# A four-heads-a-step layout for one attention block, together with new scheduler settings, in a kernel of two attention blocks

## The chip, the cores and the metric

The kernel runs on one core of one Trainium2 chip. The metric is the device time of one execution in microseconds (us); lower is better. A kernel's time is the median of its runs.

Names used below: PE is the matmul engine and PEld its weight loads, ACT the activation engine, DVE the vector engine, POOL a fourth engine, SP the engine that issues the DMAs (loads and stores), and SPq its queue. PSUM is the memory of the tiles that the matmuls here write (ps_... in the views), SBUF the on-chip memory of the program's other tiles. The "page" of a run is a summary of the hardware profile of one execution, its "span" the time from the first to the last instruction, and the "granted clock" the share of full speed at which PE was let run.

## The reference

Two attention blocks with separate inputs; their outputs are concatenated. Block A has 32 query heads that share 4 key/value heads, block B has 32 heads with their own keys and values. B holds eight times A's cache, and it is the block that the change touches.

```python
# A: B, Sq, D, Hq, Hkv, Sk, Dh = 16, 32, 1024, 32, 4, 1024, 128   (bf16)
# B: B, Sq, D, H,  Sk, Dh      = 16, 32, 1024, 32,    1024, 128   (bf16)
def _B_ref(x, k_cache, v_cache, wq, wo):
    q = (x @ wq).reshape(B, Sq, H, Dh).transpose(0, 2, 1, 3)
    scores = jnp.einsum("bhqd,bhkd->bhqk", q, k_cache) * (Dh ** -0.5)
    p = softmax(scores, axis=-1)
    o = jnp.einsum("bhqk,bhkd->bhqd", p, v_cache)
    return o.transpose(0, 2, 1, 3).reshape(B, Sq, H * Dh) @ wo
# A is the same with k and v repeated 8 times along the head axis
return jnp.concatenate([a, b], axis=-1)          # (16, 32, 2048)
```

## The kernel before

The program does not issue instructions directly. Every operation is recorded with what it reads and writes, and a **list scheduler** then simulates the recorded program and fixes the order of instructions on each engine. That order is final, and the chip keeps to it: in the trace of the kernel before, DVE's 884 recorded operations and ACT's 725 started in the order of the program. An engine whose next entry is not ready waits, as DVE did for 46.3 us in all before the transposes of K. The simulation has its own picture of the chip: a table of durations, an assumed data rate `DMA_BW` (bytes per us), a latency for a signal between engines, a margin before a DMA may be issued, and a window `look` within which two candidates count as equally early.

```python
A_STEPS_FRAC = 0.92            # A's steps are spread over this part of B's steps
DMA_BW = 330.7e3               # the model's data rate: 330.7 GB/s
DMA_MARGIN = {"kb_dma": 0.5, "vb_dma": 0.5, "ka_dma": 0.5, "va_dma": 0.5}
DMA_MARGIN_DEFAULT = 2.0
DUR = {"scoresB": 1.1, ..., "exp": 1.25, ..., "KBt_tr": 1.15, ...}      # us each, cut

def list_schedule(self, lat=0.12, dma_bw=DMA_BW, dma_lat=1.8, look=0.35):
    ...   # pick the engine and operation that can start first; within `look`, the longest path to the end
            if op.dma_key is not None:                    # a load or store
                xs = max(st + 0.06, dma_free[0])
                dma_free[0] = xs + op.dur / dma_bw        # op.dur is bytes here
                op.t1 = dma_free[0] + dma_lat             # when the model sees it landed
            else:
                op.t1 = st + op.dur
            for u in users[best]:                         # what waits for it
                r = op.t1 + (0.0 if same_pe else lat)
                if uo.dma_key is not None:
                    r += DMA_MARGIN.get(uo.name, DMA_MARGIN_DEFAULT)
                ...
```

B is worked in 128 steps. A step takes two batches and two heads, 1 MiB of K and 1 MiB of V. K has two slots in SBUF and V three. A step transposes K on DVE (two transposes of 128x1024, 1223 ns each), multiplies with 32x32 PE tiles into a score buffer in PSUM, takes exp with the row sums in one ACT instruction (in the trace 1029 ns, and 200 ns for reading the accumulator), transposes the result on PE, multiplies with V and normalises. A runs 128 steps of its own between them, and the projections x@wq and the output projections are mixed in. The two score buffers rotate over A's and B's steps alike, in the order in which the steps are recorded.

```python
def quadB_all(q):
    st_ktrB(q, 0); st_ktrB(q, 1)                        # DVE transposes of K, free its slot
    if t + NKB < NIT: st_dmaK(quadsB[t + NKB])           # load of K two steps ahead
    if t >= 1 and t - 1 + NVB < NIT: st_dmaV(quadsB[t - 1 + NVB])
    st_scores(q); st_exp(q); st_ptr(q); st_pev(q, "act"); st_pv(q); ...

# K of a step: every partition gets two runs of 4 KB (t is one of two batches, hh one of two heads)
ksrc = pb["k"][q.b0:q.b0+2, q.h0:q.h0+2].rearrange("t hh (p s) d -> (hh p) t (s d)", s=16)

# score buffers
q.sbuf = sbuf_rr[0] % 2

# Q of B: project, transpose on DVE, shuffle on PE into the operand layout, and evacuate on ACT
last = e.matmul(ps_pj[:, 0:CW], xT_sb[:, 1, j, G*P:(G+1)*P], wq_sb[:, 1, j, :], ...)
pr.add("dve", lambda e: e.transpose(QBt..., Qtok...), name="QBt_tr")
for rg in range(4):
    e.matmul(ps_pj[32*rg:32*rg+32, ...], ident[32*a:32*a+32, 32*a:32*a+32], rhs, tile_position=(32*a, 32*rg))
evac(QR[:, gp, a, :, :], ps_pj[:, 0:2*Dh]..., name="QR_ev", eng="act")
```

`ps_pj` is one PSUM bank that all projections, the output projections and this shuffle share.

## Time and profile before

The kernel's three runs before the prediction had a median of 917.7 us (912.47 to 920.21).

| what | value |
|---|---|
| bytes moved | 341.64 MB |
| mean rate over the span | 375 GB/s |
| PE busy | 783.4 us, 86% of the span |
| ACT, DVE busy | 462.1 and 519.3 us |
| first 100 us | 308 GB/s |
| 100 to 840 us | 388 GB/s |

The page of the kernel before: the span, the busy time of each engine with its instructions, the rate in 40 equal slices of the span, the DMA total, the DMA queue (packets, MB, and the time of its packets as a share of 16 engines' span), and the chain of work that ended last.

```profile
span 911.5 us, 28186 instructions
...
PE 783.4 (86%) x12610; PEld 432.9 (47%) x12610; DVE 519.3 (57%) x891; ACT 462.1 (51%) x853; POOL 67.9 (7%) x76
...
GB/s 333 270 302 370 308 399 361 402 385 390 359 380 409 411 349 400 401 381 392 368 405 403 411 374 390 375 346 397 405 408 399 385 398 403 333 409 397 385 410 190
DMA packets 151934, 341.64 MB, mean 375 GB/s; under 512 B 10496, under 2 KB 26880, under 8 KB 151808
...
q1 hardware_dynamic: 151808, 339.78, 97.6%
...
PE 56%; ACT 14%; DVE 13%; DMA 12%; issue 2%; SPq 2%; POOL 0%; POOLq 0%; DVEq 0%; ACTq 0%
...
```

Two readings compete here. PE is busy for 86% of the span and makes up 56% of the chain that ended last, which looks like a PE-bound kernel. But its best slices move 411 GB/s, and at that rate 341.6 MB take 831 us (341.6 / 411, an estimate), so most of the 911.5 us is data time, with slices at 270 to 375 GB/s between the good ones.

The costliest groups of the kernel before that the change touches: line, engine, operation, output <- inputs with shapes and count | busy us, mean ns of one | idle us just before, and what ended most of it.

```profile
L848 DVE STREAM_TRANSPOSE KBt_sb<-KB_sb 128x1024 f32<-128x1024 f32 x256 | 306.6, 1223 | 46.3 <-DMA KB_sb<-in_B_k_cache_dram 22.6
L887 PE MATMUL ps_s<-KBt_sb,QR 32*32 32x512 bf16 x4096 | 167.0, 402 | 13.8 <-ACT P_sb L907 7.4
...
L907 ACT ACTIVATE P_sb<-ps_s 128x1024 bf16<-128x1024 f32 x128 | 131.7, 1029 | 70.3 <-PE ps_pt L921 36.5
...
L588 ACT CAST QR<-ps_pj 128x256 bf16<-128x256 f32 x128 | 48.5, 379 | 46.0 <-PE ps_pj L694 43.3
...
```

The same view with shapes kept apart has the Q shuffle itself on PE: 43.9 us, and 17.5 us of idle time before its matmuls.

```profile
...
L694 PE MATMUL ps_pj<-QBt,ident 32*32 32x256 bf16 x512 | 43.9, 287 | 17.5 <-ACT QR L588 10.0 <-DVE acc L748 2.6 <-DVE Qtok L590 1.5
...
```

Stretches of the kernel before: start:end, length, busy us and count of PE, PEld, DVE, ACT, POOL, then granted clock, DMA share, GB/s.

```profile
0.00:100.00 100.00, 77.32 (x800) 37.64 (x800) 34.88 (x56) 34.78 (x58) 6.45 (x16) 0.86 0.85 308
100.00:840.00 740.00, 657.45 (x10953) 371.86 (x10946) 446.98 (x772) 403.54 (x741) 61.38 (x59) 0.98 1.01 388
840.00:900.00 60.00, 45.39 (x843) 22.22 (x821) 34.93 (x57) 23.55 (x54) 0.00 (x0) 0.91 0.99 381
900.00:911.50 11.50, 3.21 (x43) 1.19 (x43) 2.48 (x8) 0.27 (x1) 0.10 (x1) 0.79 0.14 52
```

The DMA queue's own waits in the kernel before (what it waited for: us in total, times, longest). Line 813 is the load of K.

```profile
SPq L813 <- DVE KBt_sb L848: 220.4, 64, 13.0
...
```

And the waits of the engines: the K transposes on DVE waiting for K to land.

```profile
...
DVE KBt_sb L848 <- DMA KB_sb<-in_B_k_cache_dram: 22.6, 22, 2.3
...
```

A load of K cannot be issued before the slot's old contents have been transposed. Here the queue stood still for 220 us waiting for that, while the transposes themselves waited for their data for only 23 us.

The view names the DVE instruction that signalled last before the issue of the load was over, and an issue of a load of K took 0.37 us in the median (line 813), in the case below long enough for the next instruction in DVE's list to start before it and end during it. One case from the timeline of the kernel before (start, length, engine, line; other engines cut):

```profile
...
781.56 2.35 DVE L848 STREAM_TRANSPOSE KBt_sb<-KB_sb 128x1024 f32<-128x1024 f32 x2
...
783.83 0.39 DVE L949 TENSOR_TENSOR OA_sb<-ps_kt,rinv_all 128x256 bf16<-128x256 f32 x1
783.94 0.37 SPq L813 DMA_DIRECT2D KB_sb<-in_B_k_cache_dram  x1
...
```

The load starts 0.03 us after the second transpose ends (783.91), after 5.0 us of waiting, and in the program it depends on no other DVE instruction; but the view puts this wait down to line 949. So two counts are taken from the times in the traces here, load by load. The first is the queue's idle time just before loads of K: 329 us in the kernel before, all but 0.3 us of it ended by the transpose that frees the slot. The second is how long landed K waits for the start of its first transpose (a load has landed when its last signal shows in the trace): 221 us, added up over the 128 loads.

### The profile page before, as it was taken

To read this page: it belongs to the slowest core of one execution; us is meant where nothing else is said; L and a number is where in the kernel's file an instruction comes from. 1 tells how busy PE (TensorE), PEld (TensorE's weight loads), DVE (VectorE), ACT (ScalarE), POOL (GpSimd) and SP (SyncE) were. 2 spreads that over 40 slices of the span, in tenths; PEclk is the share of its full clock that TensorE was granted. 3 is DMA by queue.
4 is the path that set the end of the run, shared out by engine and by line. 5 is a ranking of instruction groups with operands and counts; after the bars stand their busy time and mean duration, and the time that the engine had idled before them with its cause. 6 is when DMAs were issued, how large, how long until landed. Compare 5 with 4: busy or idle time off the path is not lost.

```text
span 911.5 us, 28186 instructions
## 1 busy us (share of the span) xinstructions
PE 783.4 (86%) x12610; PEld 432.9 (47%) x12610; DVE 519.3 (57%) x891; ACT 462.1 (51%) x853; POOL 67.9 (7%) x76
## 2 busy tenths in 40 slices
PE   5879999999998899988898789989897888978775
PEld 2325564545554454545454455536453445545332
DVE  1415655466645566555756556666665656666553
ACT  2215665655564455655564555555554544646242
POOL 0000000100110010101010010001010100001000
PEclk7879999999999999999999999999999899989898
DMA  9789899999999999999999999999999999899995
GB/s 333 270 302 370 308 399 361 402 385 390 359 380 409 411 349 400 401 381 392 368 405 403 411 374 390 375 346 397 405 408 399 385 398 403 333 409 397 385 410 190
DMA packets 151934, 341.64 MB, mean 375 GB/s; under 512 B 10496, under 2 KB 26880, under 8 KB 151808
## 3 DMA queue, kind: packets, MB, share of 16 engines
q1 hardware_dynamic: 151808, 339.78, 97.6%
q8 instruction: 101, 1.65, 0.7%
q14 instruction: 25, 0.20, 0.1%
HBM read 337.64 MB, written 2.10 MB: 373 GB/s over the span
## 4 chain that ended last, share of the span: by engine, by line
PE 56%; ACT 14%; DVE 13%; DMA 12%; issue 2%; SPq 2%; POOL 0%; POOLq 0%; DVEq 0%; ACTq 0%
PE ps_pj L735 10%; PE ps_s L887 10%; DVE KBt_sb L848 6%; PE ps_o L971 6%; PE ps_pj L657 6%; PE ps_pt L921 6%; ACT P_sb L907 5%; PE ps_pj L674 5%; PE ps_kt L937 4%; DMA KB_sb<-in_B_k_cache_dram 4%; ACT PTA_sb L901 3%; PE ps_s L865 3%; DMA wq_sb<-in_A_wq_dram 3%; DVE acc L748 3%; PE ps_kt L839 2%
## 5 line engine op out<-in xcount | busy, mean ns | idle before, releaser
L848 DVE STREAM_TRANSPOSE KBt_sb<-KB_sb 128x1024 f32<-128x1024 f32 x256 | 306.6, 1223 | 46.3 <-DMA KB_sb<-in_B_k_cache_dram 22.6
L887 PE MATMUL ps_s<-KBt_sb,QR 32*32 32x512 bf16 x4096 | 167.0, 402 | 13.8 <-ACT P_sb L907 7.4
L901 ACT ACTIVATE PTA_sb<-ps_s 128x1024 bf16<-128x1024 f32 x128 | 131.6, 1029 | 73.1 <-PE ps_s L865 59.9
L907 ACT ACTIVATE P_sb<-ps_s 128x1024 bf16<-128x1024 f32 x128 | 131.7, 1029 | 70.3 <-PE ps_pt L921 36.5
L588 ACT COPY PT_sb<-ps_pt 128x512 f32<-128x512 f32 x128 | 74.9, 585 | 150.6 <-PE ps_o L971 116.5
L822 POOL COPY VAp_sb<-VA_sb 128x1024 bf16<-128x1024 bf16 x64 | 66.6, 1040 | 770.5 <-DMA VA_sb<-in_A_v_cache_dram 667.3
L921 PE MATMUL ps_pt<-id,P_sb 128*128 128x128 f32 x512 | 91.7, 302 | 18.4 <-ACT P_sb L907 16.9
L987 DVE TENSOR_SCALAR OB_sb<-ps_o,rinv_all 128x128 bf16<-128x128 f32 x128 | 44.4, 347 | 108.0 <-PE ps_o L971 107.6
L921 PEld LDWEIGHTS ps_pt<-id,P_sb 128*128 128x128 f32 x512 | 74.2, 208 | 43.2 <-ACT P_sb L907 25.2
L971 PE MATMUL ps_o<-VB_sb,PT_sb 128*32 128x128 bf16 x4096 | 84.9, 224 | 8.4 <-DMA VB_sb<-in_B_v_cache_dram 6.7
L865 PE MATMUL ps_s<-QT_sb,KTA_sb 128*128 128x256 bf16 x512 | 85.3, 275 | 4.2 <-ACT PTA_sb L901 2.2
L735 PE MATMUL ps_pj<-woB_sb,OTB_sb 128*128 128x512 bf16 x256 | 75.4, 391 | 12.9 <-DVE acc L748 5.4
L937 PE MATMUL ps_kt<-VAp_sb,PTA_sb 128*128 128x129 bf16 x1024 | 80.3, 221 | 5.4 <-ACT KTA_sb L588 2.3
L971 PEld LDWEIGHTS ps_o<-VB_sb,PT_sb 128*32 128x32 bf16 x4096 | 60.1, 98 | 52.1 <-issue 38.7
L657 PE MATMUL ps_pj<-xT_sb,wq_sb 128*128 128x512 bf16 x256 | 74.0, 406 | 11.4 <-DMA wq_sb<-in_A_wq_dram 4.2
L887 PEld LDWEIGHTS ps_s<-KBt_sb,QR 32*32 32x32 bf16 x4096 | 49.7, 90 | 67.5 <-issue 19.5
L937 PEld LDWEIGHTS ps_kt<-VAp_sb,PTA_sb 128*128 128x128 bf16 x1024 | 64.9, 98 | 31.2 <-issue 13.4
L674 PE MATMUL ps_pj<-wq_sb,xT_sb 128*128 128x512 bf16 x256 | 71.0, 391 | 4.3 <-ACT QR L588 1.8
L735 PE MATMUL ps_pj<-woA_sb,OTA_sb 128*128 128x512 bf16 x256 | 66.9, 389 | 7.4 <-DVE ost L751 4.7
L588 ACT CAST QR<-ps_pj 128x256 bf16<-128x256 f32 x128 | 48.5, 379 | 46.0 <-PE ps_pj L694 43.3
L748 DVE TENSOR_TENSOR acc<-acc,ps_pj 128x512 f32<-128x512 f32 x64 | 43.5, 680 | 44.6 <-PE ps_pj L735 44.2
L865 PEld LDWEIGHTS ps_s<-QT_sb,KTA_sb 128*128 128x128 bf16 x512 | 44.3, 98 | 32.3 <-ACT PTA_sb L901 5.8
(52 smaller groups left out, 574.0 us busy)
## 6 DMA issues: line engine op xcount, KB each, us to landing
KB_sb<-in_B_k_cache_dram SPq DMA_DIRECT2D x128, 1024.0 KB, 8.2
VB_sb<-in_B_v_cache_dram SPq DMA_DIRECT2D x256, 512.0 KB, 8.9
KA_sb<-in_A_k_cache_dram SPq DMA_DIRECT2D x64, 256.0 KB, 9.5
VA_sb<-in_A_v_cache_dram SPq DMA_DIRECT2D x64, 256.0 KB, 7.7
wq_sb<-in_B_wq_dram SPq DMA_DIRECT2D x32, 256.0 KB, 6.9
wq_sb<-in_A_wq_dram SPq DMA_DIRECT2D x32, 256.0 KB, 8.7
woB_sb<-in_B_wo_dram SPq DMA_DIRECT2D x32, 256.0 KB, 8.4
woA_sb<-in_A_wo_dram SPq DMA_DIRECT2D x32, 256.0 KB, 7.8
```

The source lines that it names most:

```text
L588: pr.add("act", lambda e: e.copy(dst_ap, src_ap), reads=reads, writes=writes, name=name + "@act", wtag=wtag, rtag=rtag)
L657: last = e.matmul(ps_pj[:, 0:tn], wq_sb[:, 0, j, hc * Dh:(hc + 1) * Dh], xT_sb[:, 0, j, t0:t0 + tn], start=(j == 0), stop=(j == DJ - 1))
L674: last = e.matmul(ps_pj[:, 0:CW], xT_sb[:, 1, j, G * P:(G + 1) * P], wq_sb[:, 1, j, :], start=(j == 0), stop=(j == DJ - 1))
L735: last = e.matmul(ps_pj[:, 0:OUTW], OT[:, gp, hh, :], wo_[:, hh, oh * OUTW:(oh + 1) * OUTW], start=(hh == 0), stop=(hh == nh - 1))
L848: pr.add("dve", lambda e: e.transpose(KBt_sb[:, sl, t_, :].bitcast(F32), KB_sb[:, rs, t_, :].bitcast(F32)), reads=[("KB", rs)], writes=[(" ...
L865: last = e.matmul(ps_s[:, sbf, c2, i * 2 * P:(i + 1) * 2 * P], KTA_sb[:, sl, c * P:(c + 1) * P], qt, start=True, stop=True)
L887: last = e.matmul(ps_s[32 * cg:32 * cg + 32, sbf, g2, :].rearrange("p (s j) -> p s j", s=16), lhsT, rhs, start=(fp == 0), stop=(fp == 3), ...
L901: pr.add("act", lambda e: e.activation(dst, src, ACTF.Exp, scale=scale), writes=BK_S[sbf] + [("PTA", q.half)], name="expA", rtag={("Sv", s ...
L907: pr.add("act", lambda e: e.activation(dst, src, ACTF.Exp, scale=scale, accum_out=stat[:, 0:1]), writes=BK_S[sbf] + ["P", "rowsum"], name= ...
L921: last = e.transpose(ps_pt32[:, m * P:(m + 1) * P], p32[:, m:Sk // 2:NPK], id32[:])
L937: last = e.matmul(ps_kt[:, qh * OA0:qh * OA0 + Dh + 1], PTA_sb[:, h, c, qh * P:(qh + 1) * P], VAp_sb[:, sl, 4 * h + c, 0:Dh + 1], start=(h ...
L971: last = e.matmul(ps_o[32 * a:32 * a + 32, 0:Dh], PT_pairs[:, c // 2, 32 * a:32 * a + 32, c % 2], VB_sb[:, kvs, a // 2, a % 2, c, :], star ...
```

## The change

Its intent: a step of B now takes four heads of one batch, one per group of 32 rows ("quadrant"). Q can then be projected directly into the layout that the score matmuls need, by taking every fourth column of wq as weights; the shuffle, its DVE transpose and its ACT evacuations disappear. K of a step becomes one contiguous run of 8 KB per partition. In exchange exp is split into two halves of 512 columns, with two row sums that two small DVE additions put together. Together with that the scheduler's settings are replaced: measured durations, a data rate of 390 GB/s, other margins, and A's steps spread over all of B's.

```diff
-A_STEPS_FRAC = 0.92
-DMA_BW = 330.7e3
+A_STEPS_FRAC = 1.0
+DMA_BW = 390e3
-DMA_MARGIN = {"kb_dma": 0.5, "vb_dma": 0.5, "ka_dma": 0.5, "va_dma": 0.5}
-DMA_MARGIN_DEFAULT = 2.0
+DMA_MARGIN = {}
+DMA_MARGIN_DEFAULT = 1.0
 DUR = {
-    "scoresB": 1.1, "scoresA": 0.45, "PT_trB": 0.50, "PVB": 0.8, ..., "qprojA": 1.8, "qprojB": 1.8, ...
+    "scoresB": 0.222, "scoresA": 0.222, "PT_trB": 0.235, "PVA": 0.312, "PVB": 0.116, ..., "qprojA": 0.434, ...
-    def list_schedule(self, lat=0.12, dma_bw=DMA_BW, dma_lat=1.8, look=0.35):
+    def list_schedule(self, lat=0.2, dma_bw=DMA_BW, dma_lat=1.8, look=0.1):
     ...
-                        last = e.matmul(ps_pj[:, 0:CW], xT_sb[:, 1, j, G * P:(G + 1) * P], wq_sb[:, 1, j, :], ...)
+                        w = wq_sb[:, 1, j, fp:CW:4]
+                        last = e.matmul(ps_pj[:, 0:NTOK], w, xT_sb[:, 1, j, :], ...)
-        def qprepB_tr(m_, G): ...      # DVE transpose of Q
-        def qprepB_sh(m_, G, a_list): ...   # PE shuffle and ACT evacuation
     ...
-                ksrc = pb["k"][q.b0:q.b0 + 2, q.h0:q.h0 + 2].rearrange("t hh (p s) d -> (hh p) t (s d)", s=16)
+                ksrc = pb["k"][q.b, q.h0:q.h0 + 4].rearrange("a (p s) d -> (a p) (s d)", s=32)
     ...
-            pr.add("dve", lambda e: e.transpose(KBt_sb[:, sl, t_, :].bitcast(F32), KB_sb[:, rs, t_, :].bitcast(F32)),
+            pr.add("dve", lambda e: e.transpose(KBt_sb[:, sl, t_, :].bitcast(F32).rearrange("p (s r i) -> p s r i", r=2, i=32),
+                                                   KB_sb[:, rs, t_, :].bitcast(F32).rearrange("p (s i r) -> p s r i", r=2, i=32)),
     ...
-                pr.add("act", lambda e: e.activation(dst, src, ACTF.Exp, scale=scale, accum_out=stat[:, 0:1]), ...)
+                for g in range(2):
+                    pr.add("act", lambda e, ...: e.activation(dst, src, ACTF.Exp, scale=scale, accum_out=st[:, g:g + 1]), ...)
+                for i in range(2):
+                    o, r = 64 * i, 64 * (1 - i)
+                    pr.add("dve", lambda e, ...: e.tensor_tensor(st[o:o + 64, 2:3], st[o:o + 64, 0:1], st[r:r + 64, 1:2], ALU.add), name="shift", ...)
```

Cut: the DUR table, the score matmuls' operands (still 32 per step of the same shape), the V load and the indexing that follows from the new step.

## The prediction

> **What bounds it now.** The kernel must move 341.6 MB (DMA line of the page). Its best 20 us slices reach 411 GB/s, so moving alone would take an estimated 831 us (341.6 MB / 411 GB/s) of the 911.5 us span. By stretch (windows view): 0 to 100 us ran at 308 GB/s with a granted clock of 0.86; 100 to 840 at 388; 840 to 900 at 381; then an 11.5 us tail with nearly no data. The losses against 411 are thus an estimated 25 us in the start, 41 in the middle, 4 to 5 in the end and 11 in the tail. The middle alternates. Sixteen 20 us slices run at 400 GB/s or more with PE busy 17.1 of 20 us: DMA-bound. Eleven run below 375 GB/s with PE busy 18.1: there PE, with the projections mixed in, is the slower one. [...]
>
> **Removed.** (1) The Q shuffle: 512 matmuls, 43.9 us busy on PE (287 ns each), with some 17.5 us of PE idle just before them (groups), mostly a wait for ACT to empty the shared projection bank (10.0 us). (2) Its evacuations: 48.5 us of ACT (128 x 379 ns). (3) The Q transpose: 14.0 us of DVE (32 x 437 ns). With them goes the use of that one PSUM bank by a third user.
>
> **Added.** (1) Exp in two halves. One exp now is 1029 ns plus 200 ns for reading the accumulator. The 128x512 ACT copy at 585 ns and the 128x1024 one at 1016 give 0.84 ns a column, so a half is an estimated 600 + 200 ns: 1.6 against 1.23 us a step, +48 us of ACT. That cancels what ACT loses. (2) Two small DVE adds a step, costed like the 160 ns reciprocal: +41 us of DVE, off the chain unless they delay a K transpose.
>
> **Moved, free.** Scores keep 32 matmuls a step (8 more cost 0.23 us in the timeline: eight tiles already share the array); K transposes keep 1.22 us, strided by 8 bytes; K arrives as 8 KB runs instead of 4 KB. Weights strided by 8 bytes should load in about 100 ns as now[...]; no trace here shows that stride yet.
>
> **Schedule.** In the old order PE does only A projections from 42 to 63 us while B's buffers stand full (timeline). The new order puts four B steps between them, which should lift the first 100 us to about 340 GB/s: -10 us. A's steps are spread over all 128 B steps instead of 92%, easing PE in the middle, but A and B now end together: up to 3 us more tail.
>
> **On the critical path.** The PE work matters only in the PE-bound slices. I take the middle from 388 to 400 GB/s: -22 us. Sum: -32 us, span about 880, time 884 us; 862 to 906 holds 8 in 10. Chances: faster by over 2% 0.82, within 2% 0.15, slower 0.03.
>
> **Right if the page shows:** PE busy 725 to 750 us, ACT 455 to 470, DVE 540 to 555; mean 383 GB/s or more; first 100 us at 330 or more; strided weight loads 95 to 110 ns; half exps near 600 ns; K transposes 1.22 us. SP still waits mostly for K transposes (now 220 us).
>
> **Wrong if:** strided loads or transposes run slower; the small adds hold back K transposes, and with them K's slots and loads; the new order leaves K or V loads late; or the middle is held at 388 by DMA itself, so that only the start gains (then about 905).

The plain weight loads of the projections, 128x128, took 99 to 101 ns in the trace of the kernel before. -10 us in the start and -22 us in the middle make the -32 us. "Eight tiles already share the array" is a reading of the timeline before: eight score matmuls took 0.43 us together and 32 took 1.14, an estimated 0.24 us for eight more, while one takes 402 ns in the mean.

## The result

| | median us | lowest to highest, 4 runs |
|---|---|---|
| before | 918.69 | 912.47 to 920.21 |
| after | 859.29 | 857.85 to 861.23 |

The ratio after/before is 0.9367 with a 95% interval of 0.9319 to 0.9415: faster by 6.3%. A ratio here is the mean time of one kernel's fast runs over the mean time of the other's fast runs of the same rounds, so it is not quite the ratio of the medians.

The page of the kernel after, with the lines that answer to those of before.

```profile
span 857.6 us, 27298 instructions
...
PE 717.3 (84%) x11970; PEld 436.2 (51%) x12098; DVE 541.5 (63%) x1115; ACT 447.1 (52%) x981; POOL 67.9 (8%) x76
...
GB/s 341 366 400 412 413 412 389 413 415 399 413 400 385 413 410 412 402 400 411 403 412 404 406 411 401 411 408 408 413 403 412 412 409 412 414 411 409 411 384 174
DMA packets 135547, 341.57 MB, mean 398 GB/s; under 512 B 10496, under 2 KB 26880, under 8 KB 119040
...
q1 hardware_dynamic: 135424, 339.78, 101.1%
...
DMA 53%; PE 19%; DVE 15%; SPq 6%; issue 4%; ACT 2%; POOL 1%; POOLq 0%; DVEq 0%
...
```

The low slices are gone: after the first two and before the last, every slice is at 384 to 415 GB/s. The chain that ended last is now 53% data and 19% PE. PE is still busy for 84% of the span, two points less than before. So the busy share of PE moved hardly at all while the time fell by 6%. About 1% of the PE's matmul records are missing from this trace (11970, where the weight loads count 12098); the same program with another setting, run e14 below, has all 12098 and 728.3 us.

The groups of the kernel after that answer to those of before, and the new small additions (line 883).

```profile
L820 DVE STREAM_TRANSPOSE KBt_sb<-KB_sb 128x1024 f32<-128x1024 f32 x256 | 306.1, 1226 | 97.7 <-DMA KB_sb<-in_B_k_cache_dram 93.9
L878 ACT ACTIVATE P_sb<-ps_s 128x512 bf16<-128x512 f32 x256 | 152.4, 600 | 84.1 <-PE ps_s L855 74.5
...
L855 PE MATMUL ps_s<-KBt_sb,QB_sb 32*32 32x512 bf16 x4096 | 146.9, 395 | 10.1 <-DVE KBt_sb L820 5.5
...
L883 DVE TENSOR_TENSOR stat<-stat 64x1 f32<-64x1 f32 x256 | 41.9, 164 | 32.0 <-ACT P_sb L878 24.4
...
```

The strided K transposes cost what the plain ones did (1226 against 1223 ns). A half exp takes 600 ns. The idle time before the K transposes doubled, and nearly all of it is now a wait for data, as it should be in a kernel bound by data.

The stretches of the kernel after, with the same columns as before.

```profile
0.00:100.00 100.00, 81.38 (x1108) 49.11 (x1124) 49.23 (x93) 48.54 (x96) 7.44 (x17) 1.00 1.02 384
100.00:790.00 690.00, 586.56 (x10029) 358.40 (x10134) 452.53 (x934) 372.51 (x825) 56.19 (x54) 0.98 1.04 407
790.00:846.00 56.00, 46.00 (x815) 27.72 (x826) 37.17 (x83) 25.76 (x63) 4.16 (x4) 0.94 0.99 385
846.00:858.00 12.00, 3.36 (x35) 0.97 (x22) 2.53 (x7) 0.27 (x1) 0.10 (x1) 0.65 0.14 51
```

The waits of the DMA queue in the kernel after (line 785 is the load of K).

```profile
SPq L785 <- DVE KBt_sb L820: 108.3, 29, 8.8
SPq L785 <- DVE stat L883: 105.0, 39, 7.8
...
```

The small additions (`stat`, line 883) are named here for the reason given above: a load of K does not depend on them. Load by load, the queue waits 296 us before loads of K, all but 1 us of it ended by the transpose that frees the slot. That is not half of the 329 us before, but nearly as much.

And the engines' waits: K transposes for K.

```profile
...
DVE KBt_sb L820 <- DMA KB_sb<-in_B_k_cache_dram: 93.9, 82, 3.1
...
```

Landed K now waits only 40 us in all for its transposes, against 221 us before.

Where the time came from, counted in bytes so that the stretches compare. The first 30.8 MB (308 GB/s x 100 us) took 100 us before. After, the slices of the page (21.44 us each) reach 30.8 MB at 81.5 us: 18 us less. The following 310 MB took 800 us before, at 388 GB/s, and 764 us after (81.5 to 846 us), at 406: 36 us less. The end with hardly any data took 11.5 us before and 12 us after. The sum is the difference of the two spans, 54 us. So the gain is a higher data rate in start and middle, and the question is what raised it.

### The profile page after: what moved, and what is told of

Same layout as the page of the kernel before. It is cut to its first block, busy times and chain, and to the rows that moved or that the text cites. A ratio compares the mean times of both kernels' runs of the same rounds, so it can differ in the third digit from the quotient of the medians.

```text
span 857.6 us, 27298 instructions
## 1 busy us (share of the span) xinstructions
PE 717.3 (84%) x11970; PEld 436.2 (51%) x12098; DVE 541.5 (63%) x1115; ACT 447.1 (52%) x981; POOL 67.9 (8%) x76
## 2 busy tenths in 40 slices
DMA packets 135547, 341.57 MB, mean 398 GB/s; under 512 B 10496, under 2 KB 26880, under 8 KB 119040
## 3 DMA queue, kind: packets, MB, share of 16 engines
q1 hardware_dynamic: 135424, 339.78, 101.1%
## 4 chain that ended last, share of the span: by engine, by line
DMA 53%; PE 19%; DVE 15%; SPq 6%; issue 4%; ACT 2%; POOL 1%; POOLq 0%; DVEq 0%
DMA KB_sb<-in_B_k_cache_dram 40%; DVE KBt_sb L820 12%; DMA VA_sb<-in_A_v_cache_dram 5%; PE ps_pj L709 4%; PE ps_s L855 3%; DMA woA_sb<-in_A_wo_dram 3%; PE ps_pj L651 3%; PE ps_pj L668 2%; SPq L800 2%; PE ps_o L947 2%; PE ps_kt L913 2%; SPq L682 1%; PE ps_s L838 1%; PE ps_pt L897 1%; DMA woB_sb<-in_B_wo_dram 1%
## 5 line engine op out<-in xcount | busy, mean ns | idle before, releaser
L820 DVE STREAM_TRANSPOSE KBt_sb<-KB_sb 128x1024 f32<-128x1024 f32 x256 | 306.1, 1226 | 97.7 <-DMA KB_sb<-in_B_k_cache_dram 93.9
L878 ACT ACTIVATE P_sb<-ps_s 128x512 bf16<-128x512 f32 x256 | 152.4, 600 | 84.1 <-PE ps_s L855 74.5
L855 PE MATMUL ps_s<-KBt_sb,QB_sb 32*32 32x512 bf16 x4096 | 146.9, 395 | 10.1 <-DVE KBt_sb L820 5.5
L897 PE MATMUL ps_pt<-id,P_sb 128*128 128x128 f32 x512 | 105.5, 305 | 9.3 <-ACT P_sb L878 7.3
L947 PE MATMUL ps_o<-VB_sb,PT_sb 128*32 128x128 bf16 x4096 | 81.6, 221 | 23.7 <-DMA VB_sb<-in_B_v_cache_dram 16.6
L897 PEld LDWEIGHTS ps_pt<-id,P_sb 128*128 128x128 f32 x512 | 82.7, 206 | 35.2 <-ACT P_sb L878 17.7
L838 PE MATMUL ps_s<-QT_sb,KTA_sb 128*128 128x256 bf16 x512 | 82.2, 275 | 3.0 <-DVE KTA_sb L584 2.0
L855 PEld LDWEIGHTS ps_s<-KBt_sb,QB_sb 32*32 32x32 bf16 x4096 | 49.3, 90 | 60.9 <-DVE KBt_sb L820 10.6
L709 PE MATMUL ps_pj<-woB_sb,OTB_sb 128*128 128x512 bf16 x206 | 62.0, 394 | 16.6 <-ACT OTB_sb L582 4.5
L668 PE MATMUL ps_pj<-xT_sb,wq_sb 128*128 128x512 bf16 x234 | 64.2, 389 | 8.4 <-DMA wq_sb<-in_B_wq_dram 3.4
L651 PE MATMUL ps_pj<-xT_sb,wq_sb 128*128 128x512 bf16 x232 | 63.9, 380 | 8.3 <-DMA wq_sb<-in_A_wq_dram 4.1
L883 DVE TENSOR_TENSOR stat<-stat 64x1 f32<-64x1 f32 x256 | 41.9, 164 | 32.0 <-ACT P_sb L878 24.4
```

Source lines behind the costliest of these rows:

```text
L651: last = e.matmul(ps_pj[:, 0:tn], wq_sb[:, 0, j, hc * Dh:(hc + 1) * Dh], xT_sb[:, 0, j, t0:t0 + tn], start=(j == 0), stop=(j == DJ - 1))
L668: last = e.matmul(ps_pj[:, 0:NTOK], w, xT_sb[:, 1, j, :], start=(j == 0), stop=(j == DJ - 1))
L709: last = e.matmul(ps_pj[:, 0:OUTW], OT[:, gp, hh, :], wo_[:, hh, oh * OUTW:(oh + 1) * OUTW], start=(hh == 0), stop=(hh == nh - 1))
L820: pr.add("dve", lambda e: e.transpose(KBt_sb[:, sl, t_, :].bitcast(F32).rearrange("p (s r i) -> p s r i", r=2, i=32), KB_sb[:, rs, t_, :]. ...
L838: last = e.matmul(ps_s[:, sbf, c2, i * 2 * P:(i + 1) * 2 * P], KTA_sb[:, sl, c * P:(c + 1) * P], qt, start=True, stop=True)
L855: last = e.matmul(ps_s[32 * cg:32 * cg + 32, sbf, g, :].rearrange("p (sh cl j) -> p sh cl j", sh=4, cl=4), lhsT, kt[32 * a:32 * a + 32, g, ...
```

## The experiments

Three explanations were to be told apart first. The prediction's: less work on PE, and the shuffle's waits on the shared bank gone. The first rival: the scheduler's settings, which reorder every engine and which the prediction hardly costed. The second rival: K's longer runs, which would make the same bytes cheaper to move.

Eighteen kernels ran; all gave correct results. In each call the kernel before ran too, on the same chip. The table gives all of them; the texts below quote the expectations before each call. "Start" is the rate in the first 100 us and "middle" the rate from 100 to 790 us, in GB/s; "queue before K loads" is the queue's idle time just before loads of K and "landed K waiting" the time from a load's landing to its first transpose, both counted load by load as explained above; "transposes for data" is the K transposes' wait for K in the view. All three are in us in total. Each of these comes from the one profiled execution of the run.

| run | median us | before, same call | ratio, 95% interval | start | middle | queue before K loads | transposes for data | landed K waiting |
|---|---|---|---|---|---|---|---|---|
| before | 918.69 | | | 308 | 389 | 329 | 23 | 221 |
| after | 859.29 | 918.69 | 0.937 (0.932 to 0.942) | 384 | 407 | 296 | 94 | 40 |
| e1 old layout, all new settings | 873.19 | 917.57 | 0.952 (0.947 to 0.958) | 358 | 401 | 241 | 92 | 84 |
| e2 new layout, all old settings | 897.28 | 917.57 | 0.980 (0.974 to 0.986) | 325 | 398 | 339 | 5 | 257 |
| e3 after, K in 4 KB runs | 868.22 | 917.57 | 0.946 (0.940 to 0.951) | 383 | 402 | 266 | 101 | 33 |
| e4 after, with a shuffle | 862.57 | 917.57 | 0.940 (0.935 to 0.946) | 380 | 407 | 244 | 87 | 31 |
| e5 before, even spread only | 918.55 | 916.24 | 1.001 (0.994 to 1.008) | 329 | 380 | 353 | 20 | 190 |
| e6 before, data rate only | 909.74 | 916.24 | 0.994 (0.987 to 1.000) | 317 | 388 | 284 | 91 | 342 |
| e7 before, durations only | 949.15 | 916.24 | 1.038 (1.029 to 1.047) | 317 | 375 | 354 | 23 | 294 |
| e8 before, margins, latency, look only | 902.10 | 916.24 | 0.984 (0.978 to 0.990) | 338 | 390 | 321 | 33 | 176 |
| e9 e1 without the data rate | 908.56 | 917.53 | 0.990 (0.983 to 0.997) | 347 | 385 | 337 | 28 | 166 |
| e10 e1 without the durations | 875.58 | 917.53 | 0.955 (0.949 to 0.962) | 375 | 402 | 277 | 123 | 87 |
| e11 e1 without margins, latency, look | 883.53 | 917.53 | 0.964 (0.957 to 0.970) | 348 | 398 | 306 | 64 | 119 |
| e12 e1 without the even spread | 883.51 | 917.53 | 0.964 (0.957 to 0.971) | 330 | 403 | 276 | 95 | 106 |
| e13 after, rate 330.7 | 897.46 | 919.08 | 0.977 (0.969 to 0.986) | 343 | 390 | 366 | 13 | 194 |
| e14 after, rate 410 | 857.87 | 919.08 | 0.934 (0.926 to 0.942) | 378 | 407 | 295 | 114 | 29 |
| e15 e12 with private score buffers | 878.60 | 919.08 | 0.958 (0.950 to 0.966) | 349 | 402 | 268 | 105 | 75 |
| e16 after, spread 0.97, private buffers | 858.94 | 919.08 | 0.937 (0.929 to 0.945) | 385 | 408 | 299 | 63 | 57 |
| e17 e13, model sees K 4 us earlier | 904.76 | 917.21 | 0.987 (0.982 to 0.992) | 322 | 391 | 325 | 43 | 176 |
| e18 after, model sees K 4 us later | 908.35 | 917.21 | 0.990 (0.984 to 0.995) | 383 | 391 | 135 | 24 | 253 |

### First call: layout against schedule

**e1** is the kernel before with all the new settings; durations of operations that only the old layout has come from its own trace.

```diff
 # kernel before
-A_STEPS_FRAC = 0.92
-DMA_BW = 330.7e3
+A_STEPS_FRAC = 1.0
+DMA_BW = 390e3
-DMA_MARGIN = {"kb_dma": 0.5, ...}; DMA_MARGIN_DEFAULT = 2.0
+DMA_MARGIN = {}; DMA_MARGIN_DEFAULT = 1.0
-DUR = {"scoresB": 1.1, ..., "Qshuf": 0.25, ..., "QR_ev@act": 0.31, ...}
+DUR = {"scoresB": 0.23, ..., "Qshuf": 0.22, ..., "QBt_tr": 0.437, "QR_ev@act": 0.379}
-    def list_schedule(self, lat=0.12, ..., look=0.35):
+    def list_schedule(self, lat=0.2, ..., look=0.1):
```

> The old head layout and Q shuffle, with the new scheduler settings (measured duration table, equal DMA margins, A's steps over all B steps, DMA rate 390). Theory S (the prediction mis-sized the schedule; the order alone fills the data queue): 875 to 890 us, first 100 us at 360 GB/s or more, middle near 400 GB/s. Rival L (the shuffle's work on PE, ACT and its PSUM bank was what held the middle at 388): 900 us or more, the start better but the middle still below 395 GB/s. Rival R (8 KB runs of K raise the rate of the DMA itself): middle best slices stay at 411.

**e2** is the reverse: the changed kernel with all the old settings.

```diff
 # kernel after
-A_STEPS_FRAC = 1.0
-DMA_BW = 390e3
+A_STEPS_FRAC = 0.92
+DMA_BW = 330.7e3
 # ... and margins, DUR, lat and look likewise back to the old values; exp at 0.8 and shift at 0.165 kept
```

> The new layout with the old scheduler settings. Theory S: 895 us or more, with a poor start (under 330 GB/s in the first 100 us). Rival L: 870 to 880 us, middle near 405 GB/s, only the start lost. Rival R: the best slices reach 414.

**e3** is the changed kernel with K in two 4 KB runs per partition. A gap of 64 bytes between the halves in SBUF breaks the 8 KB run. The order of instructions on every engine is the same as in the changed kernel.

```diff
-        KB_sb = sb("KB_sb", [P, NKB, 2, 16 * Dh], BF)
+        KB_sb = sb("KB_sb", [P, NKB, 2, 16 * Dh + 32], BF)
-                ksrc = pb["k"][q.b, q.h0:q.h0 + 4].rearrange("a (p s) d -> (a p) (s d)", s=32)
+                ksrc = pb["k"][q.b, q.h0:q.h0 + 4].rearrange("a (p i s) d -> (a p) i (s d)", i=2, s=16)
 # ... load and transpose take [..., 0:16 * Dh]
```

> The changed kernel with K's buffer padded between its halves, so that K lands in runs of 4 KB as before; the order on every engine is the same. Rival R: 866 us or more and a middle of 403 GB/s or less. Theories S and L: within 2 us of the changed kernel, about 859.

**e4** is the changed kernel with a shuffle put back that has no use: four 256-column matmuls into the shared bank and their ACT evacuation in every step of B.

```diff
+        def dummy_shuffle(t):
+            def e_sh(e):
+                for rg in range(4):
+                    rhs = xT_sb[0:32, 1, 0, 0:2 * Dh].rearrange("p (hp x) -> p hp x", hp=2)
+                    last = e.matmul(ps_pj[32 * rg:32 * rg + 32, 0:2 * Dh]..., ident[0:32, 0:32], rhs, start=True, stop=True, tile_position=(0, 32 * rg))
+                return last
+            pr.add("pe", e_sh, reads=[("xT", 1, 0), "ident"], writes=[BK_PJ], name="Qshuf")
+            evac(QD[:, t % 2, :, :], ps_pj[:, 0:2 * Dh]..., name="QR_ev", eng="act", ...)
     for t in range(NIT):
         ...
+            dummy_shuffle(t)
```

> The changed kernel with the old shuffle's work put back as dummy work (4 matmuls of 256 columns into the shared projection bank and one ACT evacuation a step). Rival L: 875 us or more, the middle falling toward 395 GB/s. Theory S: PE has room in the new order, so 865 us or less and a middle of 403 or more.

Measured: the new settings alone took 44 us off (873.19 against 917.57), the new layout alone 20 us (897.28; a ratio of 0.980, so clear of the noise, but it may be a little more or less than 2%), and both together 58 us (859.29; it did not run in this call, and its own ratio to the kernel before is 0.937). Under the new settings the layout is thus worth 14 us. Of these, e3 gives back 9 us (868.22) and e4 3 us (862.57); these two differences are between calls, in which the kernel before took 917.57 and 918.69 us. The remaining 2 us are not assigned to anything, and how the 20 us under the old settings divide was not measured. The kernel after stayed within 857.85 to 861.23 us in its runs; e3's lay between 864.45 and 868.88 and are clearly apart, e4's between 860.93 and 864.04 and overlap them slightly, so that "about 3 us" is at the edge of what these runs resolve.

The page and the stretches of e1 show that PE relief is not the mechanism. First its busy line and its chain:

```profile
...
PE 750.4 (86%) x12610; PEld 441.0 (50%) x12610; DVE 512.4 (59%) x891; ACT 460.5 (53%) x853; POOL 67.9 (8%) x76
...
DMA 44%; PE 32%; DVE 12%; issue 4%; SPq 3%; ACT 2%; POOL 1%; POOLq 0%; DVEq 0%
...
```

Its stretches:

```profile
0.00:100.00 100.00, 78.66 (x928) 41.63 (x929) 41.57 (x65) 39.52 (x68) 7.44 (x17) 0.90 0.97 358
100.00:790.00 690.00, 608.32 (x10558) 362.28 (x10565) 423.43 (x739) 383.64 (x715) 54.10 (x52) 0.98 1.03 401
...
```

All 12610 matmuls of the kernel before are there, shuffle included, and PE is busy for 86% of the span as before. Yet the middle runs at 401 GB/s and the start at 358. Of the 37 stretches of 20 us between 100 and 840 us, 10 were below 375 GB/s in the kernel before; in e1 it is 1. PE's busy time did fall by 33 us (783.4 to 750.4) with the same matmuls, so one could think that the gain is a PE that gets through faster. But this time does not go with the kernel's: PE is busy for 748.7 us in e9 and for 752.1 in e11 (both with about 1% of the records missing), and they take 908.56 and 883.53 us. Nor does the granted clock set the rate of the start, where it rose from 0.86 to 1.00 in the kernel after: it was 0.98 in e2 and e6 too, at 325 and 317 GB/s. PE's busy share does not tell the two kernels apart either: 86% in the one of 917 us and 86% in the one of 873 us. e4 says the same from the other side: it adds 512 matmuls, so that PE is busy for 741.2 us against 728.3 in e14's complete trace, and ACT for 483.4 against 447.1, and pays 3 us.

For e3, the queue's line and the DMA total:

```profile
...
DMA packets 151932, 341.58 MB, mean 394 GB/s; under 512 B 10496, under 2 KB 26880, under 8 KB 151808
...
q1 hardware_dynamic: 151808, 339.78, 101.1%
...
```

The packets' time fills the same share, 101.1%, of a span that is longer; multiplied out it is 877 us against 867. So in both kernels the queue is full, and the 16385 additional packets of K (151932 - 135547) cost time of their own: 8.9 us x 16 engines / 16385 packets is an estimated 8.7 ns each.

### Second call: one setting at a time on the kernel before

```diff
 # e5                          # e6                      # e7                              # e8
-A_STEPS_FRAC = 0.92           -DMA_BW = 330.7e3         -DUR = {old durations}            -DMA_MARGIN = {... 0.5}, default 2.0; lat=0.12, look=0.35
+A_STEPS_FRAC = 1.0            +DMA_BW = 390e3           +DUR = {measured durations}       +DMA_MARGIN = {}, default 1.0; lat=0.2, look=0.1
```

> The kernel before with one setting changed: A's steps spread over all B steps (1.0 for 0.92). Theory F (the even spread is what relieved PE in the middle): 895 us or less. Rival B or D (see the next two runs): 908 to 920 us.

> The kernel before with one setting changed: the data rate that the scheduler's model assumes, 390 for 330.7 GB/s. The model then stops believing that data is the only limit and orders PE's work to the pace that the chip shows. Theory B: 895 us or less, most of the 44 us that all settings gave together. Rivals D and F: 905 us or more.

> The kernel before with only the duration table replaced by durations measured in its own trace. Theory D (wrong durations misplaced the work): 895 us or less. Rivals B and F: 908 us or more, as the model still believes in 330.7 GB/s.

> The kernel before with only the margins before data issues (1.0 us for all in place of 0.5 and 2.0), the assumed signal latency (0.2 for 0.12) and the window for ties (0.1 for 0.35) changed. Theory M (the tie window lets the list scheduler pull low-priority or late work ahead): 895 us or less. Rivals B, D and F: 908 us or more.

Measured, in medians against the 916.24 us of the same call: +2, -7, +33 and -14 us. The sum is some +15 us; together they give -44. No setting does it alone, and the measured durations alone make the kernel 3.8% slower. Measured durations beside the rate of 330.7 lose; in the set with 390 they do not (third call). The queue's wait before K loads grew from 329 to 354 us with them, and landed K waits 294 us instead of 221.

### Third call: leave one out

Each run is e1 without one of the four settings, so that the question is asked where the others are present.

```diff
 # e9                          # e10                              # e11                                        # e12
-DMA_BW = 390e3                -DUR = {measured durations}        -DMA_MARGIN = {}, default 1.0; 0.2, 0.1      -A_STEPS_FRAC = 1.0
+DMA_BW = 330.7e3              +DUR = {old durations}             +DMA_MARGIN = {... 0.5}, 2.0; 0.12, 0.35     +A_STEPS_FRAC = 0.92
```

> The old layout with all new settings except the data rate, which stays 330.7. Theory C (the assumed data rate and the assumed durations must agree; each was inflated by about a fifth before, and true durations with a false rate cost 33 us): 905 us or more. Rival P (the tie window, latency and margins do most): 885 us or less.

> The old layout with all new settings except the duration table, which stays inflated. Theory C: 890 us or more. Rival P: 885 us or less, near the sum of the single effects of the others (918 less 14 less 7, some 896).

> The old layout with the new data rate, durations and even spread, but the old margins, latency and tie window. Theory C: rate and durations together carry the gain, so 885 us or less. Rival P: 895 us or more.

> The old layout with all new settings except that A's steps still end at 92% of B's. Theories C and P: within 6 us of all settings together (873). If the even spread matters once the order is good: 880 us or more.

Measured against e1's 873.19 (of the first call; the kernel before differs by 0.04 us between the two): leaving out the data rate costs 35 us, the margins with latency and `look` 10 us, the even spread 10 us, and the durations 2 us, which is within the noise. The data rate is by far the largest. The durations, which the change's own description puts forward, are hardly needed.

The stretch of e9 beside that of e1 shows the rate's part, which lies mostly in the middle (385 against 401 GB/s).

```profile
...
100.00:790.00 690.00, 576.37 (x9864) 347.64 (x9964) 404.12 (x699) 365.83 (x673) 53.07 (x51) 0.97 1.01 385
...
```

e12 puts the even spread's part in the start: 330 GB/s against e1's 358, while its middle, at 403, is as good.

```profile
0.00:100.00 100.00, 75.42 (x842) 40.60 (x852) 36.93 (x60) 37.06 (x64) 7.56 (x17) 0.88 0.88 330
...
```

### Fourth call: the data rate in the new layout, and why the spread matters

```diff
 # e13 (after)            # e14 (after)            # e15 (e12)                       # e16 (after)
-DMA_BW = 390e3           -DMA_BW = 390e3          -q.sbuf = sbuf_rr[0] % 2          -A_STEPS_FRAC = 1.0;  q.sbuf = sbuf_rr[0] % 2
+DMA_BW = 330.7e3         +DMA_BW = 410e3          +q.sbuf = 1 - q.pi                +A_STEPS_FRAC = 0.97; q.sbuf = 1 - q.pi
```

> The changed kernel with only the model's data rate set back to 330.7. If the rate is the largest part in the new layout as in the old: 885 us or more, K transposes again late (queue waits on them near 200 us). If the relief of PE in the new layout makes the order forgiving: 870 us or less.

> The changed kernel with the model's data rate at 410, the chip's best rate. If the model only has to be no slower than the chip: 854 to 862 us. If 390 is a narrow optimum: 868 us or more.

> The old layout with all new settings but A's steps at 92%, and with the two score buffers fixed: one for A, one for B. Theory V (the even spread helped the start because strict alternation makes the rotating buffers private): 100 us at 355 GB/s or more and 876 us or less. Rival (the even load itself matters): start near 330 GB/s or a total of 880 us or more.

> The changed kernel with private score buffers and A's steps ending at 97% of B's, so that A's last projections are out of the tail. If the tail is the sum of both programs' endings: 852 to 857 us. If the tail is B's own chain: 858 to 862 us.

Measured: with the model's rate back at 330.7 GB/s and nothing else changed, the kernel after takes 897.46 us, 38 us more. That is as much as with all old settings (e2, 897.28). In the new layout the other settings therefore bring nothing without the rate; whether the rate alone would bring all of it was not run. With 410 it takes 857.87 us (855.25 to 860.58), within the noise of 859.29. So of the three rates tried, 390 and 410 are alike, and 330.7 loses; the kernel after moves 398 GB/s in the mean. Where between 330.7 and 390 the loss begins was not tried.

The chain of e13 and its middle:

```profile
...
PE 50%; DVE 17%; DMA 16%; ACT 10%; SPq 4%; issue 3%; DVEq 0%; POOLq 0%
...
```

```profile
...
100.00:790.00 690.00, 577.64 (x9629) 339.26 (x9627) 438.92 (x888) 356.52 (x780) 54.10 (x52) 0.98 1.01 390
...
```

This is the kernel after, without a shuffle, and its chain reads "PE 50%, DMA 16%" like that of the kernel before. One number in the scheduler's model decides whether this kernel looks bound by PE or by data. The PE has the same work to do in both.

e15 and e16 test why spreading A's steps evenly helps. The score buffers rotate over all steps, so at 1.0, where A and B alternate strictly, each block always gets the same buffer. At 0.92 there are places with two steps of A in a row, and the buffers change hands. (Building the kernel after with a buffer forced on each block gives the identical instruction order, which confirms the reading for 1.0.) With private buffers at 0.92, e15 recovers 5 of the 10 us (in medians; the intervals of the ratios overlap), and its start is 349 GB/s, between 330 and 358.

```profile
0.00:100.00 100.00, 80.04 (x919) 43.58 (x919) 40.21 (x62) 40.24 (x67) 8.37 (x18) 0.97 0.94 349
...
```

So the hand-over of buffers is probably about half of that effect; the rest is left unexplained. In the new layout, 0.97 with private buffers is as good as 1.0 (e16, 858.94). The new layout at 0.97 with rotating buffers was not run.

### Fifth call: is it the place of the K transposes?

The last columns of the table suggest a mechanism. DVE works its list in order (its 884 operations in the trace before and 1108 after). If the model thinks that data comes slowly, it believes that K lands late, and puts each K transpose late in DVE's list, behind instructions that wait for PE. Then K stands landed, its slot is not freed, and the queue stalls. In all runs of the first four calls at the low rate (the kernel before, e2, e5, e7, e8, e9, e13) the transposes wait 5 to 33 us for data, and landed K waits 166 to 294 us for them; in the runs at 390 or 410 it is 63 to 123 us and, but for e6, 29 to 119. The queue's wait before K loads differs less, 321 to 366 against 241 to 306 us. e6 has the new rate and hardly any of the gain; its transposes wait 91 us for data like the good runs', but its landed K waits 342 us, so by that column it belongs to the slow ones. To test whether this is enough, e17 keeps the low rate and lets only the K transposes see their data 4 us earlier. e18 keeps the right rate and lets them see it 4 us later.

```diff
 # in list_schedule, for each user uo of op
                 r = op.t1 + (0.0 if same_pe else lat)
+                if op.name == "kb_dma" and uo.name == "KBt_tr":
+                    r += -4.0        # e17, with DMA_BW = 330.7e3;   e18: r += 4.0, with 390e3
```

> The changed kernel with the model's rate at 330.7, but with the model letting a K transpose start 4 us before its data lands in the model. Theory K (the low rate hurts because K transposes are placed too late and hold K's two slots): most of the 38 us comes back, 875 us or less, VectorE waits for K data in 50 steps or more. Rival (the low rate hurts through the order of PE or of the loads at large): 888 us or more.

> The changed kernel at 390, but with the model letting a K transpose start only 4 us after its data lands in the model. Theory K: 872 us or more, VectorE waits for K data in fewer than 40 steps and the data queue waits longer for K transposes. Rival: within 5 us of the changed kernel.

Measured: e17 takes 904.76 us, no better than e13's 897.46. That is the rival's number, but it does not decide, because on the chip the edit hardly moved the transposes. Landed K still waits 176 us for them (194 in e13), the queue waits 325 us before K loads (366), and the transposes wait for data in 28 steps, where theory K had asked for 50 or more:

```profile
...
DVE KBt_sb L822 <- DMA KB_sb<-in_B_k_cache_dram: 42.9, 28, 6.0
...
```

e18 takes 908.35 us, 49 us more than the kernel after. Here the transposes did move: landed K waits 253 us for them instead of 40, and they wait for data in only 22 steps, as theory K had said. But the queue's wait before K loads did not grow; it fell to 135 us, while its wait before loads of V grew from 49 to 229 us. The view has the larger part of that as a wait for the multiplication with V, which frees V's slots:

```profile
SPq L802 <- PE ps_o L949: 141.6, 60, 7.3
...
```

So late K transposes are enough to cost as much as the low rate does (e18), and the queue's wait then shows up at the next buffer. Whether they are what costs at the low rate is not shown, since e17 did not bring them forward. What speaks for it is the last column: landed K waits 29 to 119 us in all kernels that take 884 us or less, and 166 to 342 us in all that take 897 us or more. That is a match over twenty kernels and not a test. Which instructions carry the loss at the low rate stays open.

What could not be tried: a third slot for K would loosen the tie between transposes and loads, but that kernel does not build: its buffers do not fit in SBUF (in a build of the kernel after with three slots, a buffer that needs 256 bytes per partition finds 160 left). No experiment gave a version that clearly beats the kernel after; e14 and e16 are within its noise. At 413 GB/s, which many of its slices reach, its 341.6 MB would take an estimated 827 us.

## Why the prediction was right or wrong

The direction was right, but the size was not: 884 us was predicted with a range of 862 to 906, and 859.29 was measured, below the range. That it was faster at all is due mostly to the settings (44 us in e1), of which the prediction costed only the order in the start (-10 us), so the right direction was in part luck.

- **"... which should lift the first 100 us to about 340 GB/s: -10 us."** Mis-sized: 384 GB/s, and 18 us by bytes. The reason given, a better mix of A and B in the start, is only part of it. In the old layout the new settings bring 308 to 358; without the even spread it is 330 (e12). The new layout adds the rest, to 384.
- **"The PE work matters only in the PE-bound slices. I take the middle from 388 to 400 GB/s: -22 us."** This is the step that failed. The middle went to 406 GB/s over the bytes of the account above, and 36 us came off. The mechanism was another one: with all PE work left in (e1) the middle reaches 401 GB/s, and with the work removed but the model's rate at 330.7 (e13) it stays at 390. The slices below 375 GB/s with PE busy for 18.1 of 20 us were read as bound by PE. With all the PE work left in and only the order changed (e1), one of ten slices below 375 GB/s between 100 and 840 us is left; with the work removed but the model's rate at 330.7 (e13) there are seven. So it was the order, and not the amount of PE work, that made them slow.
- **The data rate in the model** was not costed at all. The text's paragraph on the schedule names the order in the start and the spread, and passes over the one setting that was worth 35 us in the old layout (e9) and 38 in the new one (e13).
- **"Moved, free: ... K arrives as 8 KB runs instead of 4 KB."** Not free but a gain: 9 us (e3), the largest part of what the layout brought.
- **The removed shuffle.** Its parts were read correctly from the trace, but only an estimated 3 us of them were on the path in the new order (e4), not most of 22. In the old order this was not measured.
- **Exp in two halves, "+48 us of ACT. That cancels what ACT loses".** The half exp at 600 ns was right. The sum of the parts came out as predicted, with reads of the accumulator at 203 ns: (600 + 203) x 256 - (1029 + 200) x 128 is 48 us. But ACT is busy for 447 us, below the predicted 455 to 470, because most of the time of these reads overlaps the activations beside them: by the traces they add only 9 us of their 52 to the busy time after, and 4 of 26 before. The groups of ACT after add up to 511 us.
- **Small adds, "+41 us of DVE, off the chain unless they delay a K transpose".** 41.9 us, and DVE's 541.5 us lies in the predicted 540 to 555. Whether they cost time was not tested. Of the 105 us that the view puts down to them (the line with `stat` above), 92 are waits for K transposes by the times, and the rest falls into the issue of the loads; and landed K waits only 40 us in all for its first transposes, so they hold these back by no more than that.
- **PE busy 725 to 750 us:** 717.3 in a trace with about 1% of the matmuls missing; 728.3 in e14's complete one.
- **Strided weight loads 95 to 110 ns:** missed, see the two lines below. The plain loads for A are line 651, the strided ones for B line 668, in the kernel after with shapes kept apart:

```profile
...
L668 PEld LDWEIGHTS ps_pj<-xT_sb,wq_sb 128*128 128x128 bf16 x256 | 24.6, 117 | 26.6 <-issue 5.8 <-DMA wq_sb<-in_B_wq_dram 4.4 <-DVE acc L722 2.1
...
L651 PEld LDWEIGHTS ps_pj<-xT_sb,wq_sb 128*128 128x128 bf16 x256 | 21.4, 97 | 22.9 <-DMA wq_sb<-in_A_wq_dram 5.2 <-issue 2.8 <-DVE QT_sb L584 1.2
...
```

117 against 97 ns, in the same run. The loads at a stride of 4 bf16 elements took 20 ns more each than the plain ones, both of 128x128; that is 5 us in 256 loads, beside 512-column matmuls of 389 ns. That the stride would cost nothing had been an assumption, with no trace behind it. Whether it costs time was not tested.
- **"SP still waits mostly for K transposes (now 220 us)":** right: counted load by load it waits 296 us before K loads (329 before), far more than before any other load (69 us before A's V comes next). The 108 us of the view are not a halving, as shown above.
- **K transposes at 1.22 us, up to 3 us more of a tail, a mean of 383 GB/s or more:** right (1.226 us; under 1 us; 398 GB/s).

## What to carry to other kernels

In a kernel whose order is fixed ahead by a model, check the model's data rate against what the chip delivers. Here 330.7 against a delivered 398 GB/s cost 35 to 38 us once the other settings were right, more than all removed work together (an estimated 3 us); corrected alone, on the kernel before, it brought only 7. A slice with a busy PE and a low data rate is not yet PE-bound; look at how long landed data waits to be used (221 us before, 40 after; the queue's own wait for free slots told little, 329 and 296), and settle it by changing only the order or by putting the work back. When a view names what ended a wait, check it once against the times and the program's dependencies. Test settings by leaving each one out of the full set as well as alone, for they interact: the measured durations alone lost 33 us, and within the set they were worth 2, no more than noise.
